# Fused windowed attention and ReGLU FFN: q and k of the second and third halves by casting loads and TensorE transposes, with a new order of the first stages

## The chip, the cores and the metric

The kernel runs on one core of one Trainium2 chip. The time is the device time of one execution in microseconds (us), the median of several runs. The profile is one execution with the hardware profiler; its span is a little shorter than the time. PE is TensorE, PEld its weight loads, DVE is VectorE, ACT is ScalarE, POOL is GpSimd, and SP is SyncE, which here only issues transfers. A "q" behind an engine's name is its queue of issued work.

## The reference, cut to what matters

```python
batch, n_heads, seq, head_dim = (4, 8, 768, 64)      # q, k, v in float32
n_global, n_local = (8, 96)

scores = scale * np.matmul(q, k.transpose(0, 1, 3, 2))
rel = pos[:, None] - pos[None, :]
is_global = pos[None, :] < int(n_global)
is_local = (rel >= 0) & (rel < int(n_local))
keep = is_global | is_local
dist = np.where(is_global & ~is_local, float(n_local), np.abs(rel))
scores = scores + (-slopes[:, None, None] * dist)    # one slope for each head
scores = np.where(keep, scores, -1e9)
a = softmax(scores)
x = matmul(a, v)                                     # -> (3072 tokens, 512)

gate = np.maximum(x @ w_gate, 0.0)                   # w_gate, w_val: 512 x 1536
val = x @ w_val
out = (gate * val) @ w_out                           # w_out: 1536 x 512
```

Each query sees the first 8 keys and the 96 keys up to its own. The output of all heads is the input of a feed-forward network (FFN) with a gate.

## The kernel before

The 3072 tokens are cut into eight "halves" of 384 (s = 0 to 7; two for each batch). A half goes through attention, four head pairs p = 0 to 3, and then through the FFN (f1: gate and value products, f2: output products). [...]`weave` puts pieces of one attention between the products of another FFN. Attention needs q and k with the head dimension on the partitions, so each has to be cast to bf16 and transposed. There are two ways for this. For s = 0 and 1, an engine casts and TensorE transposes into PSUM, from where VectorE copies to kT and qT:

```python
    def load_qk_after(s, by_pairs=False):
        qs_of[s] = stage.tile([128, H, NN * D], FP32, name="qs")
        ks_of[s] = stage.tile([128, H, NN * D], FP32, name="ks")
        step = 2 if by_pairs else H
        for t in (qs_of[s], ks_of[s]):
            nc.vector.memset(t[0:1, 0:H:step, 0:1], 0.0)    # holds the load back to here
        for h in range(0, H, step):
            load_qk(s, h, h + step)                         # SyncE, float32

    def piece_t(s, p):
        qk = cast_of[s, p]
        tp = av_psum.tile([128, 512], FP32, name="av_ps")
        tp = tp[:, 0:QH].bitcast(BF16).rearrange("d (i t) -> d i t", i=2)
        tp_of[s, p] = tp
        for i in (1, 0):
            for n in range(NN):
                nc.tensor.matmul(tp[:, i, n * 128 : (n + 1) * 128], lhsT=qk[:, i, n],
                                 rhs=ident, is_transpose=True, ...)

    def piece_copy(s, p):
        b, half = divmod(s, 2)
        tp = tp_of[s, p]
        put_keys(nc.vector.tensor_copy, nc.vector.tensor_copy, kT[b % 2][p], tp[:, 1, :], half)
        for e in range(2):
            r = slice(64 * e, 64 * e + 64)
            nc.vector.tensor_copy(qTb[s % 2][r, p, e, :], tp[r, 0, :])
```

From s = 2 on, GpSimd casts, the DMA engines transpose, and GpSimd puts the keys in order:

```python
    def early_pieces(s):
        out = [(0.0, lambda p=p: piece_cast_k(s, p)) for p in range(HP)]     # GpSimd
        out += [(0.0, lambda n=n: piece_xk(s, n)) for n in range(NN)]        # SyncE, DMA transpose
        out += [(0.0, lambda p=p: piece_cast_q(s, p)) for p in range(HP)]    # GpSimd
        out += [(0.0, lambda n=n: piece_xq(s, n)) for n in range(NN)]        # SyncE, DMA transpose
        out += [(0.0, lambda p=p: piece_order(s, p)) for p in range(HP)]     # GpSimd
        return out
```

V and the weights are cast on the way in, by transfers that GpSimd issues. In vbuf, columns of ones stand beside V, for the sums of the softmax. The first 8 keys ("globals") of a batch are in every tile of its V:

```python
    def load_v(b, j, r0=0, r1=KT):
        nc.gpsimd.dma_start(out=v_dst(b, NG + r0, NG + r0 + n, j), in_=v[b, :, ...])

    def load_v_half(s):
        b, half = divmod(s, 2)
        if half == 0:
            load_v_globals(b)          # GpSimd
            spread_v_globals(b)        # SyncE, SBUF to SBUF, six of them
        for j in range(4) if half == 0 else range(4, NT):
            load_v(b, j)

    def load_w(dst, src, f0, f1):
        nc.gpsimd.dma_start(out=dst, in_=src[:, f0:f1].rearrange("(c p) f -> p c f", p=128))
```

The scores of a pair come in two forms. Where masks are not ready, `piece_bias` adds the bias with matmuls and `piece_biased` adds the scores and takes the exponential; elsewhere `piece_qk` takes the exponential and VectorE multiplies by a mask. `piece_av_wide` forms the sums and the product with V, and `piece_norm_wide` divides: ScalarE's logarithm and exponential, and VectorE's product into xT. The order of the first stages:

```python
    for p in range(HP):
        load_qk(0, 2 * p, 2 * p + 2)
    ...
    load_v_globals(0)
    for j in range(4):
        load_v(0, j)
    load_w_group(0)
    ...                                   # attention of s = 0: pairs 0, 1
    piece_biased(0, 1)
    piece_bias(0, 2)
    piece_t(0, 2)
    piece_copy(0, 2)
    cast(0, 3, V, V)
    copy_v_globals(V, 0, 1, 4)
    piece_t(0, 3)
    piece_bias(0, 3)
    piece_biased(0, 2)
    piece_copy(0, 3)
    piece_av_wide(0, 0)
    piece_norm_wide(0, 0)
    load_qk_after(1, True)
    piece_biased(0, 3)
    ...                                   # AV of pairs 1 to 3, with parts of F0[0:3] between
    zero_q(P, 1)
    ...                                   # memsets on GpSimd
    for j in range(4, NT):
        load_v(0, j)
    load_w_group(1)
    for p in range(HP):
        cast(1, p, P, P)
    load_w_group(2)
    ...                                   # attention of s = 1 between F0[0:12], the first FFN products
    load_qk_after(2)
    for h in (0, 1, 6, 7):
        setup_mask(h)
    load_w(wo_sb, moe_w_out, 0, DM)
    load_v_half(2)
    for p in range(HP):
        nc.gpsimd.memset(kT[1][p]..., 0)
    nc.gpsimd.memset(vbuf[1][:, NT - 1, :]..., 0)
    for i in range(2):
        nc.gpsimd.memset(qz[i]..., 0)
    for j in range(NT):
        fill_ones(nc.gpsimd, 1, j)
    load_qk(3, 0, H)
    load_v_half(3)
    weave(f1_1[G[0]] + f1_0[G[1]][4:] + f1_1[G[1]],                       # first weave
          [(0.1 + 0.1 * j, lambda j=j: fill_ones(nc.vector, 0, j)) for j in range(NT)],
          spread(early_pieces(2), 0.5, 1.0))
    weave(f1_0[G[2]] + f1_1[G[2]] + f2_0 + f2_1,                          # second weave
          spread(attention_pieces(2), 0.2, 0.92), spread(early_pieces(3), 0.1, 0.6))
    for c in range(2, NHALF):
        ...                                   # FFN of c, attention of c + 1, q and k of c + 2
```

Of the kernel before, what the change touches and what calls it, by code (L numbers as in the profile page):

```python
# [8 lines left out]
FP32 = mybir.dt.float32  # L9
# [6 lines left out]
def kernel(  # L16
# [88 lines left out]
    def load_qk(s, h0, h1):  # L105
        b, half = divmod(s, 2)
        if s not in qs_of:
            qs_of[s] = stage.tile([128, H, NN * D], FP32, name="qs")
            ks_of[s] = stage.tile([128, H, NN * D], FP32, name="ks")
        for src, dst in ((k, ks_of[s]), (q, qs_of[s])):  # L110
            nc.sync.dma_start(  # L111
                out=dst[:, h0:h1, :],
                in_=src[b, h0:h1, half * QH : (half + 1) * QH, :].rearrange(
                    "h (p n) d -> p h (n d)", n=NN))

    def v_dst(b, r0, r1, j):
        t = vbuf[b % 2][r0:r1, j, D:]
# [2 lines left out]
    def load_v_globals(b):  # L120
        nc.gpsimd.dma_start(out=v_dst(b, 0, NG, 0),
                            in_=v[b, :, 0:NG, :].rearrange("h p d -> p h d"))
# [5 lines left out]
    def copy_v_globals(eng, b, j0, j1):  # L128
        t = vbuf[b % 2][0:NG, :, D:].rearrange("p j (h z) -> p j h z", z=2 * D)[:, :, :, 0:D]
        eng.tensor_copy(t[:, j0:j1], t[:, 0:1].to_broadcast([NG, j1 - j0, H, D]))  # L130

    def load_v(b, j, r0=0, r1=KT):
        n = min(r1, S - KT * j) - r0
        nc.gpsimd.dma_start(  # L134
            out=v_dst(b, NG + r0, NG + r0 + n, j),
            in_=v[b, :, KT * j + r0 : KT * j + r0 + n, :].rearrange("h p d -> p h d"))
# [13 lines left out]
    def load_w(dst, src, f0, f1):  # L150
        nc.gpsimd.dma_start(out=dst, in_=src[:, f0:f1].rearrange("(c p) f -> p c f", p=128))

    def load_w_group(i):
        load_w(wg[i], moe_w_gate, i * GW * 128, (i + 1) * GW * 128)
        load_w(wv[i], moe_w_val, i * GW * 128, (i + 1) * GW * 128)
# [60 lines left out]
    def setup_sid(h):  # L216
        nc.scalar.activation(sid[:, h], ident, AF.Copy, bias=0.0, scale=-slopes[h] / scale)
# [42 lines left out]

    tp_of = {}

    def piece_t(s, p):
        qk = cast_of[s, p]
        tp = av_psum.tile([128, 512], FP32, name="av_ps")
        tp = tp[:, 0:QH].bitcast(BF16).rearrange("d (i t) -> d i t", i=2)
        tp_of[s, p] = tp
        for i in (1, 0):
            for n in range(NN):
                nc.tensor.matmul(tp[:, i, n * 128 : (n + 1) * 128],  # L270
                                 lhsT=qk[:, i, n],
                                 rhs=ident, is_transpose=True,
                                 start=(i == 1 and n == 0), stop=(i == 0 and n == NN - 1))

    def piece_copy(s, p):
        b, half = divmod(s, 2)
# [8 lines left out]
    def piece_bias(s, p):  # L285
        pool, name = (ff_psum, "ff_ps") if s == 0 and p % 2 else (qk_psum, "qk_ps")
        banks = [pool.tile([128, 512], FP32, name=name) for _ in range(3)]
        qk_of[s, p] = banks
        for g, bank in enumerate(banks_of_half[s % 2]):
            c = 0  # L290
            for i, (j, a, w, m) in enumerate(bank):
                for e in range(2):
                    nc.tensor.matmul(banks[g][:, c : c + NN * w], lhsT=sid[:, 2 * p + e],
                                     rhs=dd[:, 0 if j == 0 else 1, :, m : m + w],
                                     start=(i == 0 and e == 0), stop=False, skip_group_check=True)
                    c += NN * w

    def piece_biased(s, p):

        b, half = divmod(s, 2)  # L300
        kt = kT[b % 2][p]
        qd = qTb[s % 2][:, p].rearrange("d e (n p) -> d e n p", n=NN)
        es01 = es_pool.tile([128, 2, 480], BF16, name="es01")
        es2 = es_pool.tile([128, 480], BF16, name="es2")
        for g, bank in enumerate(banks_of_half[half]):
            ps = qk_of[s, p][g]
            es = es01[:, g] if g < 2 else es2
            c = 0
# [102 lines left out]
    def piece_av_wide(s, p, pool=av_psum, name="av_ps"):  # L411

        b, half = divmod(s, 2)
        todo = [t for bank in banks_of_half[half] for t in bank]
        av = [pool.tile([128, 512], FP32, name=name) for _ in range(2)]
        for what in range(2):
            av3 = av[what][:, 0:QH].rearrange("d (n p) -> d n p", n=NN)
            for i, (j, a, w, m) in enumerate(todo):
                for e in range(2):
                    es, ce = es_of[s, p, j, e]  # L420
                    z0 = D + 2 * D * (2 * p + e)
                    nc.tensor.matmul(av3[64 * e : 64 * e + 64, :, a : a + w],
                                     lhsT=ones if what == 0 else vbuf[b % 2][:, j, z0 : z0 + D],
                                     rhs=es[:, ce : ce + NN * w].rearrange("k (n p) -> k n p", n=NN),
                                     start=(i == 0), stop=(i == len(todo) - 1),
                                     skip_group_check=True)
        av_of[s, p] = av
# [91 lines left out]
    def cast(s, p, ek, eq):  # L519
        piece_cast(s, p, 1, ek)  # L520
        piece_cast(s, p, 0, eq)
# [8 lines left out]

    for h in range(H):
        setup_sid(h)
    load_v_globals(0)
    for j in range(4):
        load_v(0, j)
    load_w_group(0)
    for h in (2, 3, 4, 5):
        setup_mask(h)
    warm_up(7)
    piece_bias(0, 0)  # L540
# [6 lines left out]
    piece_t(0, 1)  # L547
    piece_biased(0, 0)
    piece_copy(0, 1)
    piece_biased(0, 1)  # L550
    piece_bias(0, 2)
    piece_t(0, 2)
    piece_copy(0, 2)
    cast(0, 3, V, V)
    copy_v_globals(V, 0, 1, 4)
    piece_t(0, 3)
    piece_bias(0, 3)
    piece_biased(0, 2)
    piece_copy(0, 3)
    piece_av_wide(0, 0)  # L560
    piece_norm_wide(0, 0)
    load_qk_after(1, True)
    piece_biased(0, 3)
    piece_av_wide(0, 1)
    piece_norm_wide(0, 1)
    piece_av_wide(0, 2, qk_psum, "qk_ps")
    piece_norm_wide(0, 2)
    copy_v_globals(V, 0, 4, NT)
    for f in F0[0:3]:
        f(0, LAST)  # L570
    piece_av_wide(0, 3)
    piece_norm_wide(0, 3)

    zero_q(P, 1)
    for p in range(HP):
# [3 lines left out]
    for j in range(4, NT):  # L579
        load_v(0, j)  # L580
    load_w_group(1)
    for p in range(HP):
        cast(1, p, P, P)
    load_w_group(2)


    def S1(p):
        if p in (0, 3):
            piece_bias(1, p)
            piece_biased(1, p)  # L590
        else:
            for g in range(3):
                piece_qk(1, p, g)

    def TC1(p):
        piece_t(1, p)
        piece_copy(1, p)

    def AV1(p):
        piece_av_wide(1, p)  # L600
        piece_norm_wide(1, p)

    for f in F0[0:3]:
        f(LAST, N_DC)
    F0[3]()
    TC1(0)
    F0[4]()
    TC1(1)
    F0[5]()
    S1(0)  # L610
    F0[6]()
    TC1(2)
    F0[7]()
    TC1(3)
    S1(1)
    AV1(0)
    S1(2)
    AV1(1)
    F0[8]()
    S1(3)  # L620
    F0[9]()
    AV1(2)
    F0[10]()
    F0[11]()
    AV1(3)
    load_qk_after(2)
    for h in (0, 1, 6, 7):
        setup_mask(h)
    load_w(wo_sb, moe_w_out, 0, DM)
    load_v_half(2)  # L630
    for p in range(HP):
        nc.gpsimd.memset(kT[1][p][:, 3, 32:128].bitcast(mybir.dt.uint32), 0)
# [3 lines left out]
        nc.gpsimd.memset(qz[i].rearrange("t n p e z -> t (n p e z)").bitcast(mybir.dt.uint32), 0)  # L636
    for j in range(NT):
        fill_ones(nc.gpsimd, 1, j)
    load_qk(3, 0, H)
    load_v_half(3)  # L640
    weave(f1_1[G[0]] + f1_0[G[1]][4:] + f1_1[G[1]],
          [(0.1 + 0.1 * j, lambda j=j: fill_ones(nc.vector, 0, j)) for j in range(NT)],
          spread(early_pieces(2), 0.5, 1.0))
    weave(f1_0[G[2]] + f1_1[G[2]] + f2_0 + f2_1,
          spread(attention_pieces(2), 0.2, 0.92), spread(early_pieces(3), 0.1, 0.6))

    for c in range(2, NHALF):
        placed = []
# [43 lines left out]
```

The softmax here doesn't subtract the row's maximum and nothing guards it: scores larger than these inputs give would overflow.

## Time and profile before

| | |
|---|---|
| time, median of 3 runs | 275.28 us (275.21 to 275.41) |
| span of the profile | 273.4 us |
| PE busy | 242.1 us, 89% |
| PEld busy | 142.5 us, 52% |
| DVE busy | 135.1 us, 49% |
| ACT busy | 157.2 us, 57% |
| POOL busy | 93.9 us, 34% |
| mean DMA rate | 125 GB/s |

In the rows by slice, the span is cut into 40 equal slices, and each digit is the busy share of a slice in tenths (9 is 90% or more). PEclk is the clock that TensorE was granted, in tenths of full speed. In the list of waits, each line gives the engine and its line of the program, what it waited for, and then the total in us, how often, and the longest. In a timeline, a row has the start in us, the length in us, the engine, the line of the program, the operation and the tiles (output <- inputs), and how many instructions are merged in it. GB/s counts a casting transfer by the bytes that it writes, which is half of those that it reads.

### The profile page before, as it was taken

To read this page: it belongs to the slowest core of one execution; us is meant where nothing else is said; L and a number is where in the kernel's file an instruction comes from. 1 tells how busy PE (TensorE), PEld (TensorE's weight loads), DVE (VectorE), ACT (ScalarE), POOL (GpSimd) and SP (SyncE) were. 2 spreads that over 40 slices of the span, in tenths; PEclk is the share of its full clock that TensorE was granted. 3 is DMA by queue.
4 is the path that set the end of the run, shared out by engine and by line. 5 is a ranking of instruction groups with operands and counts; after the bars stand their busy time and mean duration, and the time that the engine had idled before them with its cause. 6 is when DMAs were issued, how large, how long until landed. Compare 5 with 4: busy or idle time off the path is not lost.

```text
span 273.4 us, 4719 instructions
## 1 busy us (share of the span) xinstructions
PE 242.1 (89%) x1658; PEld 142.5 (52%) x1667; DVE 135.1 (49%) x339; ACT 157.2 (57%) x323; POOL 93.9 (34%) x229
## 2 busy tenths in 40 slices
PE   7475788996069999999999999999999999999994
PEld 4253555563035555665566556655665566656641
DVE  5753484653035425674368536661767166623410
ACT  7572188442027656885677567765786578744321
POOL 8950870049573800662045423740352000000000
PEclk9999599999659999999999999999999999999998
DMA  6999399987534986667376097782843210020012
GB/s 188 167 183 249 106 187 201 261 251 70 125 90 95 147 129 182 163 138 82 99 231 145 12 191 235 133 87 89 257 98 77 77 41 0 2 78 38 2 38 77
DMA packets 82263, 34.31 MB, mean 125 GB/s; under 512 B 58176, under 2 KB 79168, under 8 KB 82240
## 3 DMA queue, kind: packets, MB, share of 16 engines
q1 hardware_dynamic: 50384, 26.11, 34.1%
q0 software_dynamic: 31856, 7.91, 29.5%
q8 instruction: 13, 0.21, 0.3%
q14 instruction: 10, 0.08, 0.1%
HBM read 28.38 MB, written 6.29 MB: 127 GB/s over the span
## 4 chain that ended last, share of the span: by engine, by line
PE 64%; issue 9%; DVE 6%; POOL 6%; DMA 6%; ACT 4%; SPq 4%; POOLq 0%; ACTq 0%
PE ff_ps L459 32%; PE ff_ps L482 22%; PE av_ps L391 5%; PE qk_ps L363 4%; DMA ks<-in_k_dram 3%; DVE xT L408 3%; POOL vbuf L134 2%; SPq L111 2%; SPq L330 1%; DMA qs<-in_q_dram 1%; ACT rcp L405 1%; ACT lnd L400 1%; DVE ht L475 1%; DMA qT<-qz 1%; SPq L334 1%
## 5 line engine op out<-in xcount | busy, mean ns | idle before, releaser
L459 PE MATMUL ff_ps<-xT,wg 128*128 128x384 bf16 x384 | 80.4, 330 | 4.3 <-DVE xT L437 2.9
L459 PE MATMUL ff_ps<-xT,wv 128*128 128x384 bf16 x384 | 79.6, 330 | 0.9 <-DVE ht L475 0.3
L468 ACT ACTIVATE grelu<-ff_ps 128x384 bf16<-128x384 f32 x96 | 46.9, 490 | 39.5 <-DVE ht L475 19.5
L475 DVE TENSOR_TENSOR ht<-ff_ps,grelu 128x384 bf16<-128x384 f32 x96 | 53.3, 555 | 27.5 <-PE ff_ps L459 19.1
L482 PE MATMUL ff_ps<-wo_sb,ht 128*128 128x512 bf16 x279 | 66.5, 379 | 0.4
L366 ACT ACTIVATE es<-qk_ps 128x432 bf16<-128x432 f32 (+2 forms) x78 | 40.9, 531 | 24.3 <-PE qk_ps L363 22.8
L375 DVE TENSOR_TENSOR es<-es,m_all 128x432 bf16<-128x432 bf16 (+5 forms) x118 | 36.4, 340 | 35.4 <-ACT es L366 34.8
L459 PEld LDWEIGHTS <-wv 128*128 128x128 bf16 x384 | 36.9, 99 | 27.6 <-issue 7.0
L408 DVE TENSOR_TENSOR xT<-av_ps,rcp 64x384 bf16<-64x384 f32 x48 | 26.6, 555 | 46.7 <-ACT rcp L405 41.8
L459 PEld LDWEIGHTS <-wg 128*128 128x128 bf16 x384 | 36.5, 99 | 24.7 <-issue 2.3
L482 PEld LDWEIGHTS <-ht 128*128 128x128 bf16 x288 | 26.8, 97 | 27.6
L363 PE MATMUL qk_ps<-qT,kT 128*128 128x432 bf16 (+5 forms) x118 | 26.7, 289 | 11.3 <-DMA qT<-qz 11.3
L319 POOL CAST kc<-ks 128x384 bf16<-128x384 f32 x24 | 11.7, 535 | 54.8 <-DMA ks<-in_k_dram 54.8
L400 ACT ACTIVATE lnd<-av_ps 64x384 f32<-64x384 f32 x48 | 23.3, 485 | 12.0 <-PE av_ps L391 11.3
L487 ACT COPY osb<-ff_ps 128x512 f32<-128x512 f32 x24 | 14.1, 586 | 23.7 <-PE ff_ps L482 22.8
L134 POOL DMA_DIRECT2D vbuf<-in_v_dram x28 | 24.4, 885 | 0.5 <-DVE xT L408 0.3
L391 PEld LDWEIGHTS <-vbuf 128*128 128x128 bf16 x216 | 18.2, 98 | 8.2 <-issue 0.5
L363 PEld LDWEIGHTS <-kT 128*128 128x128 bf16 x118 | 11.4, 98 | 20.4 <-issue 12.7
L391 PE MATMUL av_ps<-es,vbuf 128*128 128x216 bf16 (+4 forms) x216 | 21.2, 226 | 0.3 <-DVE xT L408 0.2
L327 POOL CAST qz<-qs 128x192 bf16<-128x192 f32 x48 | 14.4, 349 | 2.2 <-DMA qs<-in_q_dram 2.2
L405 ACT ACTIVATE rcp<-lnd 128x384 f32<-128x384 f32 x24 | 12.5, 523 | 0.8
L316 ACT ACTIVATE es<-qk_ps 128x432 bf16<-128x432 f32 (+2 forms) x12 | 5.5, 531 | 7.0 <-PE qk_ps L311 7.0
(79 smaller groups left out, 136.9 us busy)
## 6 DMA issues: line engine op xcount, KB each, us to landing
out_dram<-osb SPq DMA_DIRECT2D x24, 256.0 KB
ks<-in_k_dram SPq DMA_DIRECT2D x6, 768.0 KB
qs<-in_q_dram SPq DMA_DIRECT2D x6, 768.0 KB
vbuf<-in_v_dram POOLq DMA_DIRECT2D x24, 120.0 KB, 4.8
ks<-in_k_dram SPq DMA_DIRECT2D x8, 192.0 KB
qs<-in_q_dram SPq DMA_DIRECT2D x8, 192.0 KB
wg<-in_moe_w_gate_dram POOLq DMA_DIRECT2D x3, 512.0 KB, 7.1
wv<-in_moe_w_val_dram POOLq DMA_DIRECT2D x3, 512.0 KB, 8.9
```

The costliest lines, as they stand in the source:

```text
L134: nc.gpsimd.dma_start(out=v_dst(b, NG + r0, NG + r0 + n, j), in_=v[b, :, KT * j + r0 : KT * j + r0 + n, :].rearrange("h p d -> p h d"))
L363: nc.tensor.matmul(ps[:, c : c + n_], lhsT=kt[:, j, :], rhs=qd[:, :, :, a : a + w], start=True, stop=True)
L366: nc.scalar.activation(es[:, 0:cols], ps[:, 0:cols], AF.Exp, bias=0.0, scale=scale)
L375: nc.vector.tensor_mul(e4, e4, mk)
L391: nc.tensor.matmul(av3[:, :, a : a + w], lhsT=vb[:, j, z0 : z0 + 128], rhs=es[:, c : c + NN * w].rearrange("k (n p) -> k n p", n=NN), star ...
L400: nc.scalar.activation(ln[o0 : o0 + 64], av[d0 : d0 + 64, 0:QH], AF.Ln, bias=0.0, scale=1.0)
L405: nc.scalar.activation(rc, ln, AF.Exp, bias=0.0, scale=-1.0)
L408: nc.vector.tensor_tensor(xT_of[s][r, p, :], av_of[s, p, e_][r, 0:QH], rc[r], op=ALU.mult)
L459: nc.tensor.matmul(st[key][:, 0:QH], lhsT=w_of(w, dc, fc), rhs=xT_of[c][:, dc, :], start=(dc == 0), stop=(dc == N_DC - 1))
L468: nc.scalar.activation(gr, psg[:, 0:QH], AF.Relu, bias=0.0, scale=1.0)
L475: nc.vector.tensor_tensor(ht[:, fc, :], psv[:, 0:QH], st["r", fc], op=ALU.mult)
L482: nc.tensor.matmul(ps2, lhsT=ht[:, fc, n * 128 : (n + 1) * 128], rhs=wo_sb[:, fc, :], start=(fc == 0), stop=(fc == N_FC - 1))
```

## The change

q and k of the second half (s = 1) and of the third (s = 2) no longer come in as float32 through SyncE's queue with a cast on GpSimd. A casting transfer that GpSimd issues writes bf16 directly, so these loads stand in one queue with V and the weights: s = 1 ahead of the first weights, s = 2 behind the last group of gate and value weights and ahead of w_out. TensorE transposes both halves, with each head of a pair by itself (64 columns), because the casting load keeps the heads apart. For the third half this takes the place of GpSimd's casts, the DMA transposes and GpSimd's ordering of the keys. Attention of s = 1 follows right behind attention of s = 0, before the FFN of s = 0 begins, to use times when TensorE has little to do. The loads of s = 3 are placed in the middle of the first weave, and the pieces of attention of s = 2 are spread over an earlier part of the second.

```diff
+    def load_qk_cast(s, parts=2):
+        b, half = divmod(s, 2)
+        n = H // parts
+        for i, (src, name) in enumerate(((q, "qs"), (k, "ks"))):
+            t = stage.tile([128, H, NN * D], FP32, name=name)
+            qk16[s, i] = t.rearrange("p h x -> p (h x)").bitcast(BF16).rearrange(
+                "p (h x) -> p h x", h=H)[:, :, 0 : NN * D]
+        for h in range(0, H, n):
+            for i, src in ((1, k), (0, q)):
+                nc.gpsimd.dma_start(
+                    out=qk16[s, i][:, h : h + n],
+                    in_=src[b, h : h + n, half * QH : (half + 1) * QH, :].rearrange(
+                        "h (p n) d -> p h (n d)", n=NN))
...
-    def piece_t(s, p):
+    def piece_t(s, p, pool=av_psum, name="av_ps"):
...
+                for e in range(1 if s == 0 else 2):
+                    r = slice(0, 128) if s == 0 else slice(64 * e, 64 * e + 64)
+                    src = (cast_of[s, p][:, i, n] if s == 0
+                           else qk16[s, i][:, 2 * p + e, n * D : (n + 1) * D])
+                    nc.tensor.matmul(tp[r, i, n * 128 : (n + 1) * 128],
+                                     lhsT=src, rhs=ident, is_transpose=True,
...
+    load_qk_cast(1)
     load_w_group(0)
...
+    piece_t(0, 2)
     piece_biased(0, 1)
-    piece_bias(0, 2)
-    piece_t(0, 2)
     piece_copy(0, 2)
     cast(0, 3, V, V)
     copy_v_globals(V, 0, 1, 4)
+    piece_bias(0, 2)
+    piece_biased(0, 2)
     piece_t(0, 3)
+    piece_copy(0, 3)
     piece_bias(0, 3)
-    piece_biased(0, 2)
-    piece_copy(0, 3)
-    piece_av_wide(0, 0)
-    piece_norm_wide(0, 0)
-    load_qk_after(1, True)
+    AV(0, 0)
     piece_biased(0, 3)
...
     load_w_group(1)
-    for p in range(HP):
-        cast(1, p, P, P)
     load_w_group(2)
+    load_qk_cast(2)
+    load_w(wo_sb, moe_w_out, 0, DM)
...
+    piece_t(1, 0, *QKB)
+    AV(0, 2, *QKB)
+    piece_copy(1, 0)
+    piece_t(1, 1, *FFB)
+    AV(0, 3)
+    piece_copy(1, 1)
+    S1(0)
+    copy_v_globals(V, 0, 4, NT)
+    piece_t(1, 2, *FFB)
+    piece_copy(1, 2)
+    S1(1)
+    piece_t(1, 3, *FFB)
+    piece_copy(1, 3)
+    F0[0]()
+    S1(2)
+    F0[1]()
+    F0[2]()
+    AV(1, 0)
...                                        # S1(3), AV(1, 1) to AV(1, 3) between F0[3] and F0[11]
-    load_qk_after(2)
...
-    load_qk(3, 0, H)
-    load_v_half(3)
+    T2 = [(0.0, f) for p in range(HP) for f in (lambda p=p: piece_t(2, p, *QKB), lambda p=p: piece_copy(2, p))]
     weave(f1_1[G[0]] + f1_0[G[1]][4:] + f1_1[G[1]],
-          [(0.1 + 0.1 * j, lambda j=j: fill_ones(nc.vector, 0, j)) for j in range(NT)],
-          spread(early_pieces(2), 0.5, 1.0))
+          [(0.05 + 0.06 * j, lambda j=j: fill_ones(nc.vector, 0, j)) for j in range(NT)],
+          [(0.6, lambda: load_qk_after(3)), (0.6, lambda: load_v_half(3))],
+          spread(T2, 0.55, 0.95))
     weave(f1_0[G[2]] + f1_1[G[2]] + f2_0 + f2_1,
-          spread(attention_pieces(2), 0.2, 0.92), spread(early_pieces(3), 0.1, 0.6))
+          spread(attention_pieces(2), 0.02, 0.8), spread(early_pieces(3), 0.1, 0.6))
```

S1(p) is the scores of a pair of s = 1; after the change only pair 2 takes the form with masks, before it pairs 1 and 2 did. AV(s, p) is `piece_av_wide` followed by `piece_norm_wide`.

More of the change, by code (lines that the diff above doesn't have):

```diff
@@ L114, in load_qk @@
                     "h (p n) d -> p h (n d)", n=NN))
+    qk16 = {}
+    def load_qk_cast(s, parts=2):
[11 more added lines that the diff above has]
+                        "h (p n) d -> p h (n d)", n=NN))
     def v_dst(b, r0, r1, j):
@@ L261 @@
     tp_of = {}
-    def piece_t(s, p):
-        qk = cast_of[s, p]
-        tp = av_psum.tile([128, 512], FP32, name="av_ps")
+    def piece_t(s, p, pool=av_psum, name="av_ps"):
+        tp = pool.tile([128, 512], FP32, name=name)
         tp = tp[:, 0:QH].bitcast(BF16).rearrange("d (i t) -> d i t", i=2)
@@ L269, in piece_t @@
             for n in range(NN):
[L270 to L273, printed above, removed]
+                for e in range(1 if s == 0 else 2):
[4 more added lines that the diff above has]
+                                     lhsT=src, rhs=ident, is_transpose=True,
+                                     start=(i == 1 and n == 0), stop=(i == 0 and n == NN - 1))
     def piece_copy(s, p):
@@ L532, with AV @@
         setup_sid(h)
+    QKB, FFB = (qk_psum, "qk_ps"), (ff_psum, "ff_ps")
+    def AV(s, p, *pool):
+        piece_av_wide(s, p, *pool)
+        piece_norm_wide(s, p)
     load_v_globals(0)
@@ L535 @@
         load_v(0, j)
+    load_qk_cast(1)
     load_w_group(0)
-    for h in (2, 3, 4, 5):
+    for h in range(2, 6):
         setup_mask(h)
@@ L555 @@
     copy_v_globals(V, 0, 1, 4)
+    piece_bias(0, 2)
+    piece_biased(0, 2)
     piece_t(0, 3)
+    piece_copy(0, 3)
     piece_bias(0, 3)
-    piece_biased(0, 2)
-    piece_copy(0, 3)
-    piece_av_wide(0, 0)
-    piece_norm_wide(0, 0)
-    load_qk_after(1, True)
-    piece_biased(0, 3)
[L564 to L572, printed above, removed]
+    AV(0, 0)
+    piece_biased(0, 3)
+    AV(0, 1)
     zero_q(P, 1)
@@ L581 @@
     load_w_group(1)
-    for p in range(HP):
-        cast(1, p, P, P)
     load_w_group(2)
+    load_qk_cast(2)
+    load_w(wo_sb, moe_w_out, 0, DM)
     def S1(p):
-        if p in (0, 3):
+        if p == 2:
+            for g in range(3):
+                piece_qk(1, p, g)
+        else:
             piece_bias(1, p)
             piece_biased(1, p)
[L591 to L604, printed above, removed]
+    piece_t(1, 0, *QKB)
[16 more added lines that the diff above has]
+    AV(1, 0)
     F0[3]()
-    TC1(0)
+    S1(3)
     F0[4]()
-    TC1(1)
     F0[5]()
-    S1(0)
+    AV(1, 1)
     F0[6]()
-    TC1(2)
+    AV(1, 2, *QKB)
     F0[7]()
[L614 to L618, printed above, removed]
     F0[8]()
-    S1(3)
+    AV(1, 3)
     F0[9]()
-    AV1(2)
     F0[10]()
     F0[11]()
-    AV1(3)
-    load_qk_after(2)
     for h in (0, 1, 6, 7):
         setup_mask(h)
-    load_w(wo_sb, moe_w_out, 0, DM)
     load_v_half(2)
```

## The prediction, made before the changed kernel was run

> **What bounds the kernel now.** I read the slices by time first, then the list of waits of TensorE, then the timeline of GpSimd and the chain, and last the sums by stage.
>
> From the page, the three rows that say when TensorE works, when GpSimd works and at which clock:
>
> ```profile
> PE   7475788996069999999999999999999999999994
> POOL 8950870049573800662045423740352000000000
> PEclk9999599999659999999999999999999999999998
> ```
>
> A slice is 273.4 / 40 = 6.8 us. From slice 13 (89 us) TensorE is full to the end, so that part is bound by its matmuls and only a change in their number could shorten it. Everything to be won lies before: a thin start (slices 0 to 6), and one hole (slice 10) with a slow clock behind it. The waits of TensorE name the hole, the two small losses near 27 us, and what the TensorE queue waited for:
>
> ```profile
> PE qk_ps L363 <- DMA qT<-qz: 11.3, 1, 11.3
> PE ff_ps L459 <- DVE xT L437: 2.9, 3, 1.5
> PE av_ps L270 <- DVE qk L238: 2.6, 2, 2.2
> PE av_ps L270 <- POOL qk L238: 2.3, 2, 1.5
> ```
>
> The 11.3 us are the first score matmul of the third half (s = 2), from 66.1 to 77.5 us. What made its q late is seen in the timeline of GpSimd (start, length, what; in brackets the idle time before and its cause):
>
> ```profile
> 33.42 1.05 POOL L151 DMA_DIRECT2D wo_sb<-in_moe_w_out_dram  x1
> 58.27 0.55 POOL L634 MEMSET vbuf<- 128x544 uint32 x1 [18.96 <-DMA vbuf<-vbuf]
> 61.41 2.01 POOL L139 MEMSET vbuf<- 128x288 uint32 x7
> 63.56 2.46 POOL L134 DMA_DIRECT2D vbuf<-in_v_dram  x3
> ```
>
> So it is one queue of tasks: w_out lands 15.6 us after 33.4 (its group's time to landing), at 49.0; the V globals of batch 1 stand behind it; the SyncE copies of them run from 49.2 to 55.4; the memset of vbuf waits for those until 58.27; only then come the memsets, the V issue, at 65.99 the casts of k and q, and from 67.9 six DMA transposes of 1.3 us each. The sums by stage (length, busy us of PE, PEld, DVE, ACT and POOL with counts, TensorE clock, DMA share, GB/s):
>
> ```profile
> 17.00:26.00 9.00, 5.50 (x67) 3.33 (x64) 3.39 (x8) 5.12 (x12) 0.74 (x1) 1.00 1.42 203
> 26.00:33.50 7.50, 5.19 (x33) 3.48 (x33) 3.72 (x12) 0.49 (x1) 5.42 (x11) 0.54 0.51 154
> 33.50:46.00 12.50, 11.15 (x146) 7.47 (x144) 8.08 (x26) 10.14 (x22) 5.81 (x14) 1.00 1.17 186
> 66.00:77.50 11.50, 0.16 (x2) 0.05 (x2) 0.16 (x1) 0.49 (x1) 8.56 (x28) 0.70 0.78 123
> ```
>
> Up to 46 us TensorE is idle for about 13.4 us and works at half clock from about 26 to 33 us: q and k of the second half start at 17.9 us, behind weights, and their casts on GpSimd begin at 26.3.
>
> **What the Trainium skill says.** "TensorE: Matmul & The Clock Gate", Part 1: an idle window of about 3.4 us halves the clock. The trace agrees: after the thin stretch the clock is 0.54, after the hole 0.50 (75 to 80 us), and four 384-column matmuls take 1.49 us there against 0.81. A hole thus costs more than its length. "DMA: Bandwidth & Descriptors", SWDGE vs HWDGE vs iDMA: only GpSimd's queue can cast on the way, and it has one context. The trace fits a line of waiting: what GpSimd issues lands in that order (V by 12.6 us, first gate group 16.1, first value group 18.6). The same page, Issuing engines are not separate DMA queues: SyncE's loads share the engines with it. Here the second value group took 11.3 us to land beside q and k, the third 8.2 without them. "SBUF — State Buffer", SBUF: two separate sides: VectorE and GpSimd can lock each other out. kT<-kT on VectorE took 0.26 us once and about 0.5 to 0.65 the other times, while GpSimd was busy; no run here shows the cause.
>
> **Part 1, the order of the loads.** The casting loads of s = 1 go in at about 9 us, before the first weights. One queue, so I add up landings. Rates from the trace: w_out, 3.1 MB as read, landed 8.1 us after the weights before it, 390 GB/s; plain q/k loads ran at 345 GB/s (60 to 62 us); V loads of 245 KB followed each other by 0.9 us. For the casting q/k loads with 768-byte runs I choose 330 GB/s: 1.57 MB in 4.8 us. Landings, estimated: V 12.6; q and k of s = 1 17.5 (first four heads 15); weights 0 23; V rest 25; weights 1 30.5; weights 2 36; q and k of s = 2 41; w_out 49; V of batch 1 about 53. Needed: first heads at about 18; weights 0 at 24 to 25; weights 1 at about 33. All meet it, by 1 to 3 us. GpSimd loses eight casts of 0.51 us and gets eight issues (four for each half) of about 0.6 us, scaled between 0.9 us for V's 960 runs and 0.78 for a weight group's 512; nothing waits for it there.
>
> **Part 2, the start.** Moving the scores of pair 2 ahead of the transposes of pair 3 lets ScalarE use the 3.9 us that it idled before 15.02. The following order of attention 1 has this work from 17 us: TensorE's busy time up to 46 us is 32.6, less some 3 for the half clock, so 29.5; 9.8 of it is done by 17. The 19.7 us left give 36.7 if nothing waits. ScalarE's chain (norms of three pairs 3.1, twelve exponentials 5.9, four norms 4.1, gate activations 2.9) is 16 us and VectorE's some 15, so neither is longer, but they alternate: pair 0 of s = 1 is copied only after two xT, so S1(0) cannot start before about 21.4, and AV(1,0) waits for its exponentials. I give 3.5 us to such waits, a choice: 36.7 + 3.5 = 40.2, say **40.5** for the first f1_1 matmul, which in the kernel before stands at 46.0 (behind AV(1,3)). That is 5.5 us. There the kernel before also waited 0.8 us at 46.7, behind the small memset of ks; this goes too.
>
> **Part 3, the hole.** The third half no longer passes GpSimd and the DMA transposes. Its data lands at about 41; TensorE transposes it from 48 (0.55 of a 13 us weave). The hole of 11.3 us goes, and the half clock behind it: 77.5 to 81 has three groups of four at 1.28 instead of 0.65 us and two scores, 2.3 us. Put back: 4 pieces of 12 transposes, written in two column halves. The 64-column pairs of line 422 run side by side (8 in 0.33 us), so 12 should cost what 6 of full width did, 0.34 us: 1.4 us for four pieces. VectorE gets four copies of the half-0 kind, 1.45 us each from first to last (11.04 to 12.50), one per FFN pair of 1.3 us that already needs 0.56. 2.0 against 1.65 us of TensorE: four times 0.35, about 1 us, once the buffer is full.
>
> **Sum.** 5.5 + 0.8 + 11.3 + 2.3 - 1.4 - 1.0 = 17.5. I take off 1 us more for the next wait below, and get 275.3 - 16.5 = 258.8, say **259**. What comes after, full of matmuls in both kernels, moves forward as it is.
>
> **Rivals.** First, a wait on GpSimd takes the hole's place. AV of s = 2 needs ones in vbuf, set by GpSimd after the same globals and copies. That chain loses nothing: w_out at 49, copies to 55.4, ones at 61.4 to 63.4. By my count the second weave begins at 40.5 + 13 + 1.4 + 1 = 55.9, and AV(2,0) stands at 0.24 of its 26 nominal us, with six score pieces of 0.3 before it: 55.9 + 8 = 64, so it is nearly a draw. This is also a floor: if all before went faster, AV would wait, and the total would not go below some 254 to 256. If the one queue is slower, it is worse. Second, the queue becomes the bound. If the casting loads reach only 200 GB/s, q and k take 7.8 us each: weights come 3 us later, w_out at 55, ones at 68, so 5 us are lost at AV(2,0) and 2 at the start: 266. For it: V with 128-byte runs moves 270 GB/s as read; against: these runs are three times as long. Third, attention 1 without FFN work between is a chain of latencies, with TensorE idle like 17 to 26 us now (5.5 busy of 9). Then the first weave starts at 44 and the total is 262 to 263. Fourth, the hole was hidden anyway: nothing speaks for it, as TensorE is full from there to the end.
>
> **Range and chances.** The hole is nearly sure, and alone it exceeds 2% (5.5 us). A waiting chain could give back up to 7 us; the start could give 2 more. So 254 to 267. Faster by over 2%: 0.94; within: 0.04, for two rivals together; slower: 0.02.
>
> **What would show it.** Right: no wait on qT<-qz above 1 us before the third half; the first scores of s = 2 near 56 us; clock at 1.00 from 17 us on; first f1_1 near 40. GpSimd without casts of s = 1 and s = 2. VectorE nearly full at 47 to 54 us. Wrong: TensorE waiting on DMA of ks or qs near 17 us, on wg at 24 or 33, on vbuf's memset near 62, or a clock of 0.5 after 20 us.

## The result, and the profile after

The changed kernel takes 253.26 us (252.94 to 253.57, 4 runs), against 275.35 us of the kernel before in the same series: a ratio of 0.919 (0.917 to 0.921). The prediction was 259 us with a range from 254 to 267, so the measured time lies 0.7 us below the range. The direction and the main cause were right; the start of the kernel gained almost twice what I gave it.

The rows by slice of the page of the changed kernel; a slice is now 251.2 / 40 = 6.3 us:

```profile
PE   7679999999999999999999999999999999999993
POOL 8996542059491067202527076203520000000000
PEclk9999999999999999999999999999999999999999
```

The hole in slice 10 is gone, and so is the thin stretch of slices 3 and 4. The clock never falls. TensorE is full from slice 3 (19 us) to the end, where before this began at slice 12 (82 us; the prediction counted one slice further).

The waits of TensorE of the changed kernel, all that are longer than 0.5 us, the warm-up and the setup of the masks included:

```profile
PE qk_ps L330 <- DVE qT L300: 1.3, 2, 0.9
PE ff_ps L242 <- DVE warm L190: 1.0, 1, 1.0
PE qk_ps L312 <- DVE qT L300: 0.9, 1, 0.9
PE ff_ps L330 <- DVE qT L300: 0.6, 1, 0.6
PE av_ps L441 <- ACT lnd L451: 0.6, 1, 0.6
PE av_ps L410 <- DVE xT L427: 0.6, 1, 0.6
```

There is no wait for a transfer in this list, neither for q and k nor for weights nor for V. What is left are short waits for VectorE's copies of kT and qT in the two first attentions.

The timeline of GpSimd of the changed kernel, with the rows that answer to those shown of before:

```profile
28.29 1.02 POOL L168 DMA_DIRECT2D wo_sb<-in_moe_w_out_dram  x1 [1.24 <-DMA wg<-in_moe_w_gate_dram]
53.30 0.55 POOL L648 MEMSET vbuf<- 128x544 uint32 x1 [13.78 <-DMA vbuf<-vbuf]
56.44 2.01 POOL L156 MEMSET vbuf<- 128x288 uint32 x7
58.40 2.43 POOL L151 DMA_DIRECT2D vbuf<-in_v_dram  x3
```

The chain w_out, V globals, SyncE's copies, memset is still there, and ends 5.0 us earlier (53.30 instead of 58.27). Only the third half no longer hangs on it.

The sums by stage up to the first f1_1 product, which stands at 35.83 us:

```profile
0.00:17.00 17.00, 12.77 (x159) 9.06 (x160) 12.04 (x39) 13.33 (x32) 15.65 (x32) 1.00 1.25 174
17.00:26.00 9.00, 7.68 (x97) 5.22 (x98) 8.29 (x30) 6.60 (x14) 6.84 (x10) 1.00 1.50 195
26.00:35.83 9.83, 9.83 (x121) 6.33 (x116) 4.71 (x9) 7.24 (x17) 3.62 (x5) 1.00 1.30 203
```

TensorE idles 4.2 us in the first 17 us (before: 17.00 - 10.79 = 6.2), 1.3 us in the next 9 (before 3.5), and then not at all.

The two traces, put side by side at four points that both have, give where the time went:

| us | before | after | difference |
|---|---|---|---|
| start to first f1_1 product | 46.00 | 35.83 | -10.2 |
| first weave, to its end | 14.1 | 15.6 | +1.4 |
| second weave, to the first product of FFN 2 | 43.7 | 30.9 | -12.8 |
| from there to the end of the span | 169.6 | 168.9 | -0.7 |
| span | 273.4 | 251.2 | -22.2 |

The -12.8 are the hole of 11.34 us and some 1.65 us of half clock behind it. (From 77.48 to 81.59 before, three groups of four products and four score matmuls took 4.1 us that take 2.5 at full clock.) The +1.4 are the transposes of the third half, 2.2 us, less the 0.8 us wait behind the memset of ks. Of the -0.7 at the end, 0.5 are a wait for the last xT of s = 2; it is gone with the earlier spread of the pieces, and is still there in run 1 below, which has the old spread. The rest is not assigned.

### The profile page after: what moved, and what is told of

Same layout as the page of the kernel before. It is cut to its first block, busy times and chain, and to the rows that moved or that the text cites. A ratio compares the mean times of both kernels' runs of the same rounds, so it can differ in the third digit from the quotient of the medians.

```text
span 251.2 us, 4845 instructions
## 1 busy us (share of the span) xinstructions
PE 239.8 (95%) x1741; PEld 142.5 (57%) x1749; DVE 137.1 (55%) x352; ACT 156.8 (62%) x323; POOL 88.4 (35%) x205
## 4 chain that ended last, share of the span: by engine, by line
PE 83%; DVE 7%; ACT 6%; DMA 1%; issue 1%; SPq 1%; ACTq 0%
PE ff_ps L478 45%; PE ff_ps L501 24%; PE av_ps L410 5%; PE qk_ps L382 5%; DVE xT L427 2%; DMA qs<-in_q_dram 1%; DVE ht L494 1%; ACT es L335 1%; ACT grelu L487 1%; PE av_ps L441 1%; ACT rcp L424 1%; PE qk_ps L330 1%; ACT lnd L419 1%; DVE qT L300 1%; PE qk_ps L290 1%
## 5 line engine op out<-in xcount | busy, mean ns | idle before, releaser
L478 PE MATMUL ff_ps<-xT,wv 128*128 128x384 bf16 x384 | 78.1, 326 | 0.8 <-DVE ht L494 0.3
L478 PE MATMUL ff_ps<-xT,wg 128*128 128x384 bf16 x384 | 78.1, 326 | 0.0
L478 PEld LDWEIGHTS <-wv 128*128 128x128 bf16 x384 | 36.0, 97 | 23.4 <-issue 2.1
L394 DVE TENSOR_TENSOR es<-es,m_all 128x432 bf16<-128x432 bf16 (+5 forms) x113 | 34.3, 332 | 26.0 <-ACT es L385 25.2
L506 ACT COPY osb<-ff_ps 128x512 f32<-128x512 f32 x24 | 14.1, 586 | 26.7 <-PE ff_ps L501 25.8
L338 POOL CAST kc<-ks 128x384 bf16<-128x384 f32 x20 | 10.0, 544 | 52.6 <-DMA ks<-in_k_dram 52.6
L382 PE MATMUL qk_ps<-qT,kT 128*128 128x432 bf16 (+5 forms) x113 | 25.8, 286 | 0.0
L410 PE MATMUL av_ps<-es,vbuf 128*128 128x216 bf16 (+4 forms) x216 | 21.4, 226 | 0.6 <-DVE xT L427 0.6
L346 POOL CAST qz<-qs 128x192 bf16<-128x192 f32 x40 | 12.4, 358 | 1.8 <-DMA qs<-in_q_dram 1.8
```

The source lines that it names most:

```text
L394: nc.vector.tensor_mul(e4, e4, mk)
L410: nc.tensor.matmul(av3[:, :, a : a + w], lhsT=vb[:, j, z0 : z0 + 128], rhs=es[:, c : c + NN * w].rearrange("k (n p) -> k n p", n=NN), star ...
L478: nc.tensor.matmul(st[key][:, 0:QH], lhsT=w_of(w, dc, fc), rhs=xT_of[c][:, dc, :], start=(dc == 0), stop=(dc == N_DC - 1))
```

## The experiments

My theory after the result: (a) the third half gains the hole and no more; (b) the start gains because q and k of s = 1 stand ahead of the weights in one queue that serves strictly in turn, and because attention 1 then fills the time in which the weights are still on their way. Rivals: that the casting itself is what counts, that the order of attention of s = 0 made it, or that the two parts need each other. All kernels below are the changed kernel with the edit given, unless said otherwise. Each ratio is to the kernel before as timed beside it (275.4 to 276.9 us in these series, the changed kernel at 0.916 and 0.919).

**1. The parts apart: the third half by the old way.**

```diff
-    load_qk_cast(2)
...
+    load_qk_after(2)                  # behind F0[11], as before
...
-          spread(T2, 0.55, 0.95))
+          spread(early_pieces(2), 0.5, 1.0))
...
-          spread(attention_pieces(2), 0.02, 0.8), ...
+          spread(attention_pieces(2), 0.2, 0.92), ...
```

> The changed kernel, but with q and k of the third half (s = 2) by the old way: float32 by SyncE's queue behind F0[11], casts and key order on GpSimd, DMA transposes, scores spread from 0.2 on. Theory (the chain on GpSimd ends at its own time, whatever TensorE did before): TensorE comes to the first score of s = 2 some 9 to 10 us earlier than in the kernel before, at about 55 us, but the last q lands only some 7 to 9 us earlier, near 69; a hole of 12 to 15 us at half clock behind it, total 264 to 267. The start alone would then be worth 9 to 11 us. Rival (the hole's end follows the earlier start in full): hole as before, 11.3 us, and the total 263 to 264. Second rival (w_out and the V globals bound the chain and do not move): q lands at 77, hole of 22 us, total 274: the start alone is worth nothing.

Measured: 269.86 us, ratio 0.978 (0.972 to 0.984). The first wait in TensorE's list:

```profile
PE qk_ps L382 <- DMA qT<-qz: 16.8, 1, 16.8
```

TensorE reached the first score of s = 2 at 55.2 us, as expected, but q was there only at 72.2 us, 5.3 us earlier than in the kernel before. So the hole grew from 11.3 to 16.8 us. The GpSimd chain moved by the 5.1 us by which its memset came earlier (53.18 instead of 58.27), no more. I had expected 7 to 9 us, and the total lies 2.9 us above the range of the theory. Of 10.0 us won in the start (first f1_1 at 36.0 us), about 6 were left in the total.

**2. The third half alone in the kernel before.** The edit is the other half of the change: load_qk_cast(2) behind the third weight group and ahead of w_out, T2 in the first weave, and the new spreads, with the old start.

> The kernel before, with only the third half by the new way (casting load behind the third weight group and ahead of w_out, TensorE transposes in the first weave, scores spread from 0.02 on, s = 3 loaded in the first weave); the start is untouched. Theory: the hole of 11.3 us and 1.65 us of half clock behind it go, 2.2 us of transposes and 0.3 us of waits for VectorE come: 264 to 266. With the start of the changed kernel worth 10 us by itself the two add up to what was measured, 22 us. Rival (the new way depends on the early start, as its loads come too late here): q and k of s = 2 land after 53 us, TensorE waits at the first transpose, and the total is 268 to 272.

Measured: 262.81 us, ratio 0.953 (0.948 to 0.958). The hole is gone, and no wait for the data of s = 2 has come: the first transpose is at 53.4 us. This gains 13.2 us, and the total is 1.2 us below the expected range. The trace shows where, in the stage from 26 to 33.5 us of this kernel:

```profile
26.00:33.50 7.50, 5.55 (x51) 3.66 (x51) 4.30 (x14) 2.36 (x7) 4.83 (x10) 1.00 0.50 158
```

The clock is 1.00 there, and was 0.54 in the kernel before. The waits for the casts of q and k were 0.8 and 0.9 us instead of 0.8 and 1.5, and the first f1_1 product came at 44.4 instead of 46.0 us, with the same work before it. The clock fell elsewhere in this execution, to 0.50 from about 14 to 17 us, and the first FFN product stands 0.9 us later (19.71 instead of 18.84). So 1.6 us net are gained in the old start, which this edit does not touch; why the clock fell at another place is not shown. Runs 1 and 2 together gain 6.2 + 13.2 = 19.4 us, against 22.1 to 23.5 for both at once. Add the 3.8 us that the old chain took back in run 1, and take off the 1.6 us that both runs count: that makes 21.6.

**3. The order in the queue.** The first weights are issued ahead of q and k of s = 1:

```diff
-    load_qk_cast(1)
     load_w_group(0)
+    load_qk_cast(1)
```

> The changed kernel with one pair of lines exchanged: the first gate and value weights are issued ahead of the casting loads of s = 1. Theory (one queue in order, at 360 to 390 GB/s of what is read): gate lands near 17, value near 19.5, the first heads of q near 21.5 instead of 15.2; TensorE waits 5 to 6 us at the first transpose of s = 1, and the total is 257.5 to 259.5. Rival (there is slack, as attention of s = 0 keeps the engines busy until 19 us and FFN pieces can run): at most 2 us, 255.

Measured: 259.71 us, ratio 0.941 (0.937 to 0.945), 0.2 us above the range of the theory. The first two of TensorE's waits:

```profile
PE qk_ps L290 <- DMA ks<-in_k_dram: 3.6, 1, 3.6
PE qk_ps L290 <- DMA qs<-in_q_dram: 1.3, 1, 1.3
```

The first transpose of q came at 20.96 us instead of 15.33, and part of what followed ran at half clock (12 transposes took 0.62 us instead of 0.34). The exchange of two lines thus costs about 6 us.

**4. Casting, or place in the order?** Three kernels load s = 1 as float32 by SyncE's queue and cast on GpSimd, with the order of all other work as in the changed kernel. In the first the loads stand right behind those of s = 0, held by nothing:

```diff
     for p in range(HP):
         load_qk(0, 2 * p, 2 * p + 2)
+    for p in range(HP):
+        load_qk(1, 2 * p, 2 * p + 2)
...
-    load_qk_cast(1)
     load_w_group(0)
...
+    for p in range(3):
+        cast(1, p, P, P)              # and cast(1, 3, P, P) ahead of load_w_group(1)
     zero_q(P, 1)
```

In all three kernels piece_t also takes its input of s = 1 as it takes that of s = 0, from the casts, as six full-width transposes instead of twelve of 64 columns.

> The changed kernel, but s = 1 comes in as float32 by SyncE's queue right behind s = 0, with no wait ahead of it, and GpSimd casts it (eight casts of 0.5 us, as in the kernel before); order of all other work as in the changed kernel. Theory (what counts is that q and k are early, not that the transfer casts): data complete by about 14 us, casts on GpSimd 13.5 to 17, V of tiles 4 to 6 issued 3 us later but with 4.8 us less before it in GpSimd's queue; total 252.5 to 255. Rival (the casting load is what makes it): plain loads share the engines with V and q, k of s = 0 and push those back by 2 to 3 us, and the casts hold back GpSimd's later issues: 256 to 259.

Measured: 260.00 us, ratio 0.941 (0.937 to 0.946): my theory fell, and the total is 1.0 us above even the rival's range. The first wait:

```profile
PE av_ps L443 <- DMA vbuf<-in_v_dram: 3.2, 3, 1.8
```

The four V loads of tiles 0 to 3 took 9.1 us from issue to landing (4.4 in the changed kernel), beside the plain loads: from 5 to 9 us SyncE's queue moved 1.27 MB and GpSimd's 0.01 MB (0.16 in the changed kernel). AV(0,0) waited three times. Early is not enough; it must not be ahead of V.

In the second, a small memset on VectorE behind piece_copy(0, 0) holds the loads back until V is issued:

```diff
-    load_qk_cast(1)
...
     piece_copy(0, 0)
+    load_qk_after(1, True)            # memsets of qs, ks on VectorE, then the loads
...
+    for p in range(3):
+        cast(1, p, P, P)
     zero_q(P, 1)
```

> The changed kernel with s = 1 as float32 by SyncE's queue and cast by GpSimd, as in the run before, but held back by a small memset on VectorE until V of tiles 0 to 3 is issued (about 8 us). Theory (it is the place in the order that counts: ahead of the weights, behind V; the plain queue shares the engines with the first weights instead of going ahead of them): V in time as in the changed kernel, first heads near 16 to 17, all of q and k by 19 to 20 instead of 17.4; total 254.5 to 257, that is most of the 6.7 us of the run before is regained. Rival (plain loads and casts on GpSimd are themselves what costs): 259 to 260 again.

Measured: 260.40 us, ratio 0.944 (0.941 to 0.947). V was in time, and yet nothing was regained. TensorE waited 4.2 us for VectorE's copy of pair 0, and VectorE in turn for GpSimd:

```profile
23.74 0.36 DVE L300 COPY qT<-qk_ps 64x384 bf16<-64x384 bf16 x1 [4.09 <-POOL qT L198]
```

L198 is GpSimd's clearing of qT, which stood behind casts that waited for data. This was my edit's own fault and told nothing of the loads. The third kernel puts the casts behind that clearing:

```diff
-    for p in range(3):
-        cast(1, p, P, P)
     zero_q(P, 1)
     ...                               # memsets of kT and vbuf
+    for p in range(3):
+        cast(1, p, P, P)
     for j in range(4, NT):
         load_v(0, j)
```

> As the run with plain loads behind V, but GpSimd clears qT of the odd halves, kT and vbuf before its casts of s = 1: in that run VectorE waited 4.1 us for the clearing, which stood behind casts that waited for data. Theory (the plain loads share the engines with the first weights: pair 0 of s = 1 landed at 13.7, pair 1 at 17.9, pair 2 at 22.4, where the casting loads have all landed by 17.4; so S1(0) is in time but the third pair is 2.5 us late): 256 to 257.5. Rival (the wait for the clearing was all, plain loads are as good): 253 to 254.5. Second rival (casts on GpSimd cost it all): 259 to 260.

Measured: 257.06 us, ratio 0.928 (0.924 to 0.932), within the range of the theory; the changed kernel beside it took 253.37. TensorE's first wait is now:

```profile
PE ff_ps L290 <- POOL qk L255: 3.8, 4, 1.6
```

TensorE waits four times for casts, and the casts wait for their data: those of the second pair of s = 1 ended at 18.4 and 20.3 us. With the casting loads everything of s = 1 had landed at 17.4. So plain loads in their best place cost 3.7 us more. What the casting load brings is that q and k can stand in the same queue, wholly behind V and wholly ahead of the weights, and that GpSimd has nothing to do for them afterwards. The 3.7 us are for both together; I did not separate the two.

**5. The order of attention of s = 0.** The scores of pair 2 go back behind the transposes and bias of pair 3:

```diff
     piece_bias(0, 2)
-    piece_biased(0, 2)
     piece_t(0, 3)
-    piece_copy(0, 3)
     piece_bias(0, 3)
+    piece_biased(0, 2)
+    piece_copy(0, 3)
     AV(0, 0)
```

> The changed kernel with the scores of pair 2 of s = 0 put back behind the transposes and the bias of pair 3, as in the kernel before. Theory (this order gave the first 17 us their 2 us of TensorE work more): ScalarE idles again before the exponentials of pair 2, AV(0,0) and all behind it come 1.5 to 2 us later: 254.8 to 255.5. Rival (attention of s = 1 cannot start before its first heads land at 15.2 us, so that an earlier s = 0 only makes a longer wait there): 253.0 to 253.9.

Measured: 254.05 us, ratio 0.920 (0.917 to 0.924). It lies between the two expectations, and the ratio does not tell it from the changed kernel. The trace does: the first transpose of s = 1 is at 16.82 instead of 15.16 us, and the first f1_1 product at 37.27 instead of 35.83; the span is 252.6 instead of 251.2 us. So some 1.4 us of the start are owed to this exchange, at most; the medians differ by 0.7 to 0.8 us.

**6. FFN ahead of attention 1.** F0[0] to F0[2] ahead of S1(0), the rest in its order:

```diff
+    F0[0]()
+    F0[1]()
+    F0[2]()
     S1(0)
...
-    F0[0]()
     S1(2)
-    F0[1]()
-    F0[2]()
```

> The changed kernel with the first three FFN products F0[0] to F0[2] put ahead of the scores of s = 1 (S1(0)), so that attention 1 is no longer right behind attention 0. Theory (the weights of group 0 land at 20.8 and 23.4 us, behind q and k; the order with attention first uses the time until then): TensorE waits on the value weights until 23.4 us, S1(0) moves from 17.6 to about 25; some 1.3 us of small waits in attention go; total 256 to 258. Rival (the FFN pieces fill the idle stretches of the attention and it makes no difference): 252.5 to 254.

Measured: 258.62 us, ratio 0.937 (0.934 to 0.941); the theory held, and its upper end was passed by 0.6 us. The waits:

```profile
PE ff_ps L478 <- DMA wg<-in_moe_w_gate_dram: 2.2, 1, 2.2
PE ff_ps L478 <- DMA wv<-in_moe_w_val_dram: 1.1, 1, 1.1
```

The two waits are 3.3 us; the products around them ran at half clock (1.46 us for four instead of 0.81), which makes up the rest of the additional time. Attention 1 right behind attention 0 is thus what fills the wait for the first weights.

**7. The ones for AV(2,0).** Three more memsets of qz[0] on GpSimd ahead of the ones of batch 1, timed beside the changed kernel:

```diff
+    for _ in range(3):
+        nc.gpsimd.memset(qz[0]..., 0)
     fill_ones(nc.gpsimd, 1, j)        # for all j
```

> The changed kernel with three more memsets of qz[0] (1.36 us each, 4.1 us) on GpSimd ahead of the ones of vbuf for batch 1. Theory (the first rival of the prediction, a GpSimd chain that takes the hole's place, is near, and missed by little): the ones of tiles 0 to 3 are set at about 61.7 instead of 57.6 us, AV(2,0) is due at 59.6, so TensorE waits about 2 us and the total is 1.5 to 2.5 us above the changed kernel beside it. Rival (there is ample slack, the chain bounds nothing): within 0.4 us of it.

> The changed kernel itself, on the same chip as the three runs beside it, as their measure: 253 to 254 us, ratio 0.917 to 0.922.

Measured: 256.05 us, ratio 0.926 (0.923 to 0.929), with the changed kernel beside it at 253.37 us, ratio 0.916 (0.913 to 0.920). The two waits that are new:

```profile
PE av_ps L410 <- POOL vbuf L156: 1.7, 1, 1.7
PE qk_ps L382 <- POOL kT L275: 1.0, 1, 1.0
```

AV(2,0) waited 1.7 us for the ones, near the 2 us expected. A second wait, which I had not foreseen, came from the same chain: the keys of s = 3, put in order by GpSimd, are now 1.0 us late too. Together 2.7 us, as much as the total rose. In the changed kernel the chain of GpSimd therefore has about 2 us of slack at AV(2,0): the first rival of the prediction was near, but it cost nothing.

**8. What the transposes of the third half cost.** Two groups of two pieces instead of four single ones:

```diff
-    T2 = [... for f in (lambda p=p: piece_t(2, p, *QKB), lambda p=p: piece_copy(2, p))]
+    def t_two(p):
+        piece_t(2, p, *QKB)
+        piece_t(2, p + 1, *QKB)
+    T2 = [... for p in (0, 2) for f in (lambda: None, lambda p=p: t_two(p),
+                                        lambda p=p: piece_copy(2, p), lambda p=p: piece_copy(2, p + 1))]
```

> The changed kernel with the transposes of s = 2 in two groups of two pieces instead of four single ones, all else in place. In the changed kernel a piece between FFN products takes 0.55 us from product to product, in the attention, between other 64-column matmuls, 0.34. Theory (the 0.2 us more are paid for each change between 64-column and full-width matmuls, not for each transpose): a group of two takes 0.9 us, the four pieces 1.8 instead of 2.2; the total falls by 0.3 to 0.5 us. Rival (the piece itself costs 0.55 us there): a group takes 1.1 us and the total is equal within 0.2 us.

Measured: 253.50 us, ratio 0.918 (0.913 to 0.922), equal to the changed kernel. In the timeline of TensorE of this kernel a group stands so:

```profile
44.80 0.81 PE L478 MATMUL ff_ps<-xT,wg 128*128 128x384 bf16 x4
45.54 0.36 PE L290 MATMUL qk_ps<-ident,ks 128*64 128x128 bf16 x6
45.73 0.33 PE L290 MATMUL qk_ps<-ident,qs 128*64 128x128 bf16 x6
45.90 0.33 PE L290 MATMUL qk_ps<-ident,ks 128*64 128x128 bf16 x6
46.06 0.33 PE L290 MATMUL qk_ps<-ident,qs 128*64 128x128 bf16 x6
46.33 0.82 PE L478 MATMUL ff_ps<-xT,wv 128*128 128x384 bf16 x4
```

The products issue every 0.65 us, so the group takes 46.33 - 45.45 = 0.88 us, where two single pieces take 1.1. The theory of a price for each change of width holds (0.09 us in, some 0.1 out): the first weave took 15.12 us instead of 15.57, the 0.45 us expected. The second part of it falls, as the total did not fall. The profiled execution took 255.30 us, the other three 253.46 to 253.54. In it the products wait 1.5 us for VectorE, behind the second pair of copies:

```profile
PE ff_ps L478 <- DVE ht L494: 1.9, 3, 1.5
53.43 1.32 DVE L272 COPY kT<-kT 128x56 bf16<-128x56 bf16 x1
```

This copy took 1.32 us, the same copy of the other three pieces 0.18; behind the first pair no product waited. The other executions have no trace, so what took the 0.45 us back in them stays open.

**9. Is there more in the start?** A version meant to be faster: pair 0 of s = 1 is copied ahead of xT(0,1), other banks are used for AV(0,0) and AV(0,2), and S1(0) runs ahead of AV(0,3).

```diff
-    AV(0, 0)
+    AV(0, 0, *QKB)
     piece_biased(0, 3)
-    AV(0, 1)
+    piece_av_wide(0, 1)
+    piece_t(1, 0, *QKB)
+    piece_copy(1, 0)
+    piece_norm_wide(0, 1)
...
-    piece_t(1, 0, *QKB)
-    AV(0, 2, *QKB)
-    piece_copy(1, 0)
+    piece_av_wide(0, 2, *FFB)
     piece_t(1, 1, *FFB)
-    AV(0, 3)
-    piece_copy(1, 1)
+    piece_norm_wide(0, 2)
     S1(0)
+    piece_copy(1, 1)
+    AV(0, 3)
```

> A version that may beat the changed kernel: the first pair of s = 1 is transposed and copied by VectorE ahead of the product xT(0,1), AV(0,0) goes to the three banks of the scores and AV(0,2) to those of the FFN, and S1(0) runs ahead of AV(0,3). Theory: the waits of TensorE between 17.2 and 19.4 us (0.42, 0.17 and 0.86) go, but V of tiles 4 to 6 lands near 25.5 us, just when AV(1,0) needs it now, so only a part shows: 252.0 to 253.0. Rival (no queue is near its limit, all is gained): 251.3 to 251.9.

Measured: 255.03 us, ratio 0.925 (0.922 to 0.928), slower than the changed kernel. In the text of this version GpSimd's clearing stood behind the copy of pair 0 and waited 3.6 us for it, and S1(0) waited 1.2 us for the clearing. The version with this mended has zero_q, the memsets of kT and vbuf and load_v(0, 4..) ahead of AV(0,0), and moves one copy:

```diff
-    copy_v_globals(V, 0, 4, NT)       # behind AV(0, 3)
...
     piece_copy(1, 3)
+    copy_v_globals(V, 0, 4, NT)
```

> As the reordered start, but with GpSimd's clearing of qT, kT and vbuf and its V loads again ahead of the copy of pair 0 of s = 1 in the program (in the run before, the clearing waited 3.6 us for that copy, S1(0) 1.2 us for the clearing, and V and the weights behind it were issued 3.7 us later), and with the copy of the V globals behind the copy of pair 3. Theory (the 1.3 us that TensorE still waits between 17 and 26 us come from the order of VectorE's work, not from loads): the first f1_1 product comes 0.8 to 1.3 us earlier than 35.8 us, and the total is 252.0 to 252.8. Rival (the queue of loads is at its limit there: value weights land at 23.4, V of tiles 4 to 6 at 25.5 us): TensorE waits on vbuf or wv instead, and the total is 253.0 to 253.6, no gain.

Measured: 252.61 us (252.26 to 252.95, 6 runs), ratio 0.913 (0.910 to 0.917). The time lies in the range of the theory, but the trace shows the cause that the rival named. The first FFN product came at 20.72 us, 2.1 us earlier than in the changed kernel, and then this happened, in the timeline of TensorE:

```profile
22.89 0.82 PE L478 MATMUL ff_ps<-xT,wv 128*128 128x384 bf16 x4 [0.20 <-DMA wv<-in_moe_w_val_dram]
25.89 0.32 PE L441 MATMUL av_ps<-es,vbuf 128*64 128x48 bf16 x4 [0.73 <-DMA vbuf<-in_v_dram]
```

TensorE waited for the first value weights and for the last tiles of V, and the first f1_1 product came at 35.75 us, against 35.83. The median is the lowest of all. Its interval overlaps one of the two of the changed kernel (0.913 to 0.920) and just meets the other (0.917 to 0.921). The span in the profile is the same (251.2 us), and the other five executions have 250.5 to 251.1. A gain of about half a microsecond is thus possible, and not shown. The order of VectorE's work was behind the waits that were left, and once it is changed, TensorE waits for the queue of loads instead.

## Why the prediction was wrong, point by point

**What bounds.** Right: the hole was the chain of GpSimd and the DMA transposes, and taking the third half off it removed it. Run 1 puts it back, run 2 removes it alone.

**Part 1, the order of the loads.** Right: the landings came within 0.5 us of the estimate up to the third weights, and 1.3 and 1.6 us early behind them. I had q and k of s = 1 at 15 and 17.5 us; by their times to landing they came at 15.2 and 17.4 (issues at 9.70 and 11.18, 5.5 and 6.2 us), one load of 393 KB every 1.1 us. Weights 0: expected 23, landed 23.4. Weights 2: expected 36, 35.6. q and k of s = 2: expected 41, 39.7. w_out: expected 49, 47.4. The 200 GB/s of the second rival did not come about: these loads ran at 360 GB/s as read.

**Part 2, the start.** This is the step that failed. "36.7 + 3.5 = 40.2, say 40.5 for the first f1_1 matmul"; it came at 35.83. The terms: I took 9.8 us as the work done by 17 us, where the sums by stage have 10.79 (an error in adding up: 9.8 is about the work of the first 16, which have 9.89). I named the 3.9 us in which ScalarE idled but gave the sum nothing for it; TensorE did 2.0 us more by 17 us, and run 5 shows that the order of pair 2 is worth up to 1.4 us in the trace. And I allowed 3.5 us for waits behind 17 us; there were 1.3. Against this, the work itself was 30.3 us, not 29.5. 1.0 + 2.0 + 2.2 - 0.8, and 0.3 of rounding, are the 4.7 us. The third rival, attention 1 as a chain of latencies, was the reason for the allowance. It held for the first pair alone: its copy stood behind two xT, as I had said, and TensorE waited 0.86 us for it, with the scores at 19.6 us instead of 21.4. The copies of the other three pairs (from 19.86 us on) ran while TensorE did the scores and transposes of their neighbours and the first FFN products. In run 6, with FFN products ahead of attention 1, the waits are for the weights.

**Part 3, the hole.** Right in kind, sizes slightly off. The half clock behind the hole cost 1.65 us, not 2.3; the transposes 2.2, not 1.4, since each change of width costs (run 8); VectorE's copies cost nothing that shows as a wait in the first weave, where I had put 1.0. A copy took 1.36 us, and with the product's 0.5 it just fits the 1.86 us from one group of TensorE to the next.

**The reserve for GpSimd.** The 1 us that I took off for the wait at AV(2,0) was not needed: the ones were being set from 56.4 us on, those of tiles 0 to 3 were there by about 57.6, and AV(2,0) came at 59.6. Run 7 shows a slack of about 2 us. My floor, "some 254 to 256", stood on the chain ending when it did before; it ended 5 us earlier. Of these, w_out landed 1.6 us earlier, SyncE issued its six copies in 4.5 us instead of 6.1, and the memset came 1.2 us behind the last of them instead of 2.9. The q and k loads that stood right ahead of these copies in SyncE's queue are gone; that this is the cause of the last two is not shown.

**The range.** The total misses 5.7 us: 4.7 of the start, 1.0 each of the reserve and the copies and 0.5 of the last xT, less 0.65 of the half clock and 0.8 of the transposes. 1 us of reserve, 1 us of wrong adding and 4 us of waits that did not come all had the same sign. The range reached 8 us up and 5 us down, although the one place with a plain lower bound, TensorE's own work, left room downward: 36.7 us without any wait was in the text, and the kernel went below it.

## What to carry to other kernels

In these runs, transfers that were cast on the way and went through one queue landed in the order of the program, and adding up gave their landings to within 1.6 us; so put first what the next stage needs, and fill the time until the weights come with work that needs none. An early start of one stage can be lost again at a later chain that does not move with it (here 10 us won, 6 left), so remove that chain together with the start. And when a schedule is estimated, an allowance for waits has to be worked out wait by wait, as a lump it hides the gain.

## What the runs showed of the hardware that was not expected

A change between 64-column and full-width matmuls on TensorE costs about 0.1 us each way: 12 transposes take 0.34 us among other 64-column matmuls and 0.55 between FFN products. The Trainium skill ("TensorEngine Tiling (Array Packing)", Key Properties) says that changing the tiling mode, not just the tile, drains TensorE; the trace agrees in kind, with the cost above.

GpSimd's issues of transfers came to a halt while eight were under way: w_out at 28.29 us waited for the gate weights issued at 18.89, which landed at 28.0, and each of the next three transfers waited for the one eight places before it. No run here shows whether the program or the chip sets the eight. It cost nothing, as the transfer queue stayed filled.

Where the clock falls could not be read off the length of a wait. In the kernel before it fell at about 26.2 us (0.51 between 26.25 and 26.50 us). This is ahead of the 1.5 us wait for a cast there, and no wait of the 4 us before was longer than 1.5 us, where the prediction names an idle window of 3.4. (In the hole the clock fell about 4.5 us after TensorE had stopped.) Both this kernel and run 2 wait 2.2 us for a cast from 11.0 to 13.2 us; behind it the clock fell to 0.50 in run 2, from 13.8 to 17.2 us, and stayed at 1.00 in the kernel before.
